# Head-by-head units, 128-token MLP chunks and two weights per unit in a clustered attention + MLP kernel

## The chip, the cores and the metric

The kernel runs on one core of a Trainium2 chip. That core has a matrix engine (PE, with its weight loads listed apart as PEld), a vector engine (DVE), a scalar engine (ACT), a general engine (POOL) and a queue engine (SP) that issues most transfers. The metric is the device time of one execution in microseconds. It is 1001.76 us before the change, the median of three runs.

## What is computed

```python
def _attn_ref(q, k, v, centroids):        # q, k, v: 4 x 8 x 768 x 64; centroids: 8 x 16 x 64
...
    q_assign = np.argmax(np.einsum('bhsd,hcd->bhsc', q_n, c_n), axis=-1)
    k_assign = np.argmax(np.einsum('bhsd,hcd->bhsc', k_n, c_n), axis=-1)
    mask = q_assign[:, :, :, None] == k_assign[:, :, None, :]
    scores = scale * np.matmul(q, k.transpose(0, 1, 3, 2))
    scores = np.where(mask, scores, -1000000000.0)
...
    return np.matmul(attn, v).astype(np.float32)      # attn: softmax of scores
def _moe_ref(x, w_in, w_out, s, b):       # x: 3072 x 512, w_in: 512 x 2048, w_out: 2048 x 512
    h = x @ w_in
    r = np.maximum(h, 0.0)
    g = s * (r * r) + b
    return (g @ w_out).astype(np.float32)
```

`q_n`, `k_n` and `c_n` are the rows divided by their norms. The attention output of the eight heads, put side by side, is `x`. The first function gives 24.6 thousand query rows against 768 keys each, the second is two large products.

## The kernel before

**Units.** A unit is 128 queries of one head against its 768 keys; there are 4 x 8 x 6 = 192. The list `units` runs over batch, chunk of 256 tokens (`c`), head pair (`hp`), 128-query tile in the chunk (`t`), head in the pair (`h`). So four units share a K pair before the next pair is touched, and one batch is 48 units in three chunks of 16. For each unit PE makes the scores (L462, two passes of two half rows: KA with QA, then KB with QB), DVE takes the row maximum (L471) and makes the bias of the exponential (L478), ACT takes the exponential (L481) and a 16-bit copy of it (L491), POOL subtracts that copy to get the low half (L504), a DMA transposes both halves, and five units later PE multiplies by V (L523 to L525; `px`). Numbers are kept as a high and a low fp16 half, and a product is three matmuls (high-high, high-low, low-high). The first 8 units use plain fp32, and so does the first MLP chunk.

**MLP.** A chunk of 256 tokens goes through 16 inner tiles of 128 columns (`ft`). Each unit has one step: `mlp_in` (L599, 12 matmuls of 256 columns), relu and two squares on ACT (L609, L615, L616), a subtraction on POOL (L628), and two units later `mlp_out` (L643, 6 matmuls of 512 columns into two accumulator banks). `LAG = 21` units lie between a unit and the MLP step of the same index, so a tail of MLP steps alone stands behind the last unit.

**Preparation.** K, Q and V are split into halves by generators that the loop steps once per unit. `prep_k` for batch b starts at unit 48b-20+4hp, `prep_v` at 48b-20, two `prep_q` per chunk 8 units apart. K: ACT writes the high half, DVE subtracts (L188) and copies the high half to `kb` (L332), a DMA transposes to KA; PE and DVE find the cluster of each row, written as a one-hot into `kb`, a second DMA transposes to KB. Q: the same with one scale per head pair, which takes a maximum over the partitions by way of PE (`allmax`, L98), two subtractions (L188) and a copy (L382) on DVE.

**Weights.** They come as 64-bit floats. `next(wgen)` at the end of a unit advances a four-step pipeline over 32 tiles (16 of w_in, 16 of w_out): load (`fetch`, SP), ACT rebases (L204, L206), DVE narrows (L210, L211), ACT or PE finds a bound (L217, L222) and POOL sets the sign (L224). `wsplit` then makes the fp16 halves, and the bound of all 16 tiles must be known for that.

**Order.** Python writes the program unit by unit; a list scheduler places the instructions on each engine's queue, and within a queue they run in order. In PSUM, scores have two pairs of banks, `acc` two banks, and the hidden bank `h` and the small bank `m` (`px`, `allmax`, `pk`, `pq`) one each. SBUF tiles of the tag `big` form one ring of 11.

Of the kernel before, what the change touches and what calls it, by code (L numbers as in the profile page):

```python
# [26 lines left out]
def tile_cluster_attention_mlp(ctx, tc, q, k, v, cent, w_in, w_out, s_in, b_in, out):  # L27
# [20 lines left out]
    URGENT = 20  # L48

# [5 lines left out]
    ps_m = ctx.enter_context(tc.tile_pool(name="ps_m", bufs=1, space=PSUM))  # L55
# [23 lines left out]
    last_exp = [None]  # L79

# [13 lines left out]
    def allmax(dst, src, name, bank="m"):  # L94
        n = src.shape[1]
        pm = (ps_m if bank == "m" else ps_h).tile([P, 512], F32, tag=bank, name=f"am_{name}")
        for j in range(n):
            nc.tensor.matmul(pm[:, j * P : (j + 1) * P], src[:, j : j + 1].broadcast_to([P, P]), identb, start=True, stop=True)  # L98
        V.tensor_reduce(dst, pm[:, : n * P].rearrange("p (n q) -> p n q", q=P), axis=AX.X, op=ALU.max)

# [78 lines left out]
    def split(hi, lo, src, f, early):  # L179
        if early:  # L180
            A.activation(src, src, AF.Copy, scale=f)
            last_split[1] = A.activation(hi, src, AF.Copy)
            yield
            G.tensor_tensor(lo, src, hi, op=ALU.subtract)
        else:
            last_split[1] = A.activation(hi, src, AF.Copy, scale=f)
            yield
            V.scalar_tensor_tensor(lo, src, f, hi, op0=ALU.mult, op1=ALU.subtract)  # L188
# [24 lines left out]

    def bound(d):
        w, p, ft = d["w"], d["p"], d["ft"]
        if p % 2:
            A.activation(w, w, AF.Abs, accum_out=l1[:, ft : ft + 1])  # L217
        else:
            wa = w.bitcast(BF16).rearrange("p a (f z) -> p a f z", z=2)[:, :, :, 1]
            pw = ps_h.tile([P, 512], F32, tag="h", name=f"pw_{ft}")  # L220
            for t in range(KT):
                nc.tensor.matmul(pw[:, :P], ones, wa[:, t, :], start=(t == 0), stop=(t == KT - 1))  # L222
# [40 lines left out]
    def wsplit(ft):  # L263
        while narrowed[0] < 2 * NF:
            next(wgen)
        made = []
        for w, f in ((wi[ft], glob[:, 2:3]), (wo[ft], glob[:, 5:6])):
            e = parts(weight_tile(f"w{'io'[len(made)]}s{ft}"))
            if made:
                A.activation(w, w, AF.Copy, scale=f)  # L270
                A.activation(e[:, 0], w, AF.Copy)
                G.tensor_tensor(e[:, 1], w, e[:, 0], op=ALU.subtract)
            else:
                A.activation(e[:, 0], w, AF.Copy, scale=f)
                yield
                V.scalar_tensor_tensor(e[:, 1], w, f, e[:, 0], op0=ALU.mult, op1=ALU.subtract)
            made.append(e)
        WSP[ft] = (made[0], made[1].rearrange("p e a f -> p e (a f)"))

    def column_sums():  # L280
# [5 lines left out]
        bias.append(weight_tile("bias").rearrange("p a f -> p (a f)"))  # L286
        V.tensor_scalar(bias[0], pb, glob[:, 7:8], None, op0=ALU.mult)
# [18 lines left out]
    kb_kept = const([P, 2, T, 2, D], F16, "kb")  # L306

    def prep_k(b, hp):
        kb = kb_kept
        if b == 0 and hp > 0:  # L310
            kb = sb.tile([P, 2 * T, P], F16, tag="big", name=f"kb_{hp}", bufs=BIGN).rearrange("p (h t) (e d) -> p h t e d", h=2, e=2)
        n = f"{b}_{hp}"
        kn = sb.tile([P, 2, T, D], F32, tag="kv", name=f"kn_{n}", bufs=5)
# [9 lines left out]
        allmax(sm[1], km, f"k{n}", "m" if b or not hp else "h")  # L323
# [8 lines left out]
        last_split[0] = V.tensor_copy(kb[:, :, :, 0, :], ka[:, :, :, 0, :])  # L332
# [6 lines left out]
        pa = (ps_m if b or not hp else ps_h).tile([P, 512], F32, tag="m" if b or not hp else "h", name=f"pk_{n}")  # L339
# [11 lines left out]
    def prep_q(b, c, hq):  # L351
        n = f"{b}_{c}_{hq}"
        nh = 4
        qn = sb.tile([P, 2 * T * P // 2], F32, tag="big", name=f"qn_{n}", bufs=BIGN)[:, : nh * CT * D].rearrange("p (h t d) -> p h t d", h=nh, t=CT)
        load(
            qn, q[b, nh * hq : nh * hq + nh].rearrange("h (p t) d -> p h t d", t=T)[:, :, c * CT : (c + 1) * CT, :]
# [3 lines left out]
        sm = sb.tile([P, 4, 2], F32, tag="qsm", name=f"qsm_{n}", bufs=3)  # L360
        qm = columns(2, f"q{n}")
        absmax(qm, qn.rearrange("p (j h) t d -> p j (h t d)", j=2))
        if b + c:
            yield
        allmax(sm[:, 1, :], qm, f"q{n}", "m" if b or c else "h")
# [7 lines left out]
        qb = sb.tile([P, 2 * T * P], F16, tag="big", name=f"qb_{n}", bufs=BIGN)[:, : nh * CT * 2 * D].rearrange("p (h t e d) -> p h t e d", h=nh, t=CT, e=2)
        both = []
        for j in range(2):
            hs = slice(2 * j, 2 * j + 2)
            both.append(split(qb[:, hs, :, 0, :], qa[:, hs, :, 0, :], qn[:, hs], sm[:, 2, j : j + 1], b + c == 0))
        for z in zip(*both):
            yield
        for z in both:  # L380
            next(z, None)
        V.tensor_copy(qa[:, :, :, 1, :], qb[:, :, :, 0, :])  # L382
        QA = sb.tile([P, nh * CT, P], F16, tag="QA", name=f"QA_{n}", bufs=2)
        QB = sb.tile([P, nh * CT, P], F16, tag="QB", name=f"QB_{n}", bufs=2)
# [422 lines left out]
```

## Time and profile before

| | us |
|---|---|
| runs | 997.03, 1001.76, 1005.69 |
| median | 1001.76 |
| profiled execution, its span | 998.5 |
| last exponential starts | 923.6 |

The profile is one execution: the busy time of each engine, a strip of 40 slices of the span, DMA queues, the chain of work that ended last, and the costliest groups of instructions. A group's row names line, engine, operation, what it writes and reads, its count, its busy time, the mean in ns of one, and the idle time before it with what ended that. A windows row gives start and end, length, then busy us and count of PE, PEld, DVE, ACT and POOL, the granted clock of PE as a share of full speed, the DMA share and GB/s. Rows for a source line alone have the busy time and count of that line instead of the engines. Busy PE is not PE at its peak: matmuls are pipelined, and a mean duration such as 276 ns for L599 is longer than the distance between two starts.

The DMA queues of the page show that small packets make up the traffic: 415760 of 448122 packets are under 512 B, and the queue took a 75.4% share of 16 engines' span.

### The profile page before, as it was taken

The page shows a single profiled execution, that of the slowest core. Times are in us where ns is not written, and L with a number is a line of the kernel's source. Part 1 is how long each engine was busy: PE and PEld are TensorE (multiplying, and loading weights), DVE is VectorE, ACT ScalarE, POOL GpSimd, SP SyncE. Part 2 cuts the span into 40 slices and gives each one's busy share as a digit, 9 for nine tenths or more (in the row PEclk, how much of TensorE's full clock was granted, in tenths as well). Part 3 has the DMA queues.
Part 4 walks back from the last instruction along what each step waited for, and adds up shares of the span by engine and source line. Part 5 has one row for each costly group of instructions (what it writes and reads, how often), then busy time and mean ns, then how long its engine had stood idle before and what let it go on. Part 6 is the DMA issues. An engine that isn't in the chain of part 4 may idle for free. (4 is left out here: it accounts for less than half of the span.)

```text
span 998.5 us, 22264 instructions
## 1 busy us (share of the span) xinstructions
PE 857.4 (86%) x8536; PEld 593.9 (59%) x8536; DVE 683.9 (68%) x1688; ACT 681.3 (68%) x1232; POOL 523.7 (52%) x498
## 2 busy tenths in 40 slices
PE   1487558978988999987899999987998998999997
PEld 0366345554655676654666666664666675767764
DVE  6887798887988567677878666588877577474100
ACT  3466678677777587765767777765877776777543
POOL 1115666534677366644456666553566565666321
PEclk9857579989999999998999999998999999999999
DMA  7855999966587787899697878898979868687300
GB/s 184 194 155 124 240 203 215 231 137 123 118 138 117 143 145 132 173 189 164 131 175 134 146 125 165 153 188 169 166 132 168 138 109 163 121 138 133 55 27 22
DMA packets 448122, 146.82 MB, mean 147 GB/s; under 512 B 415760, under 2 KB 444432, under 8 KB 448016
## 3 DMA queue, kind: packets, MB, share of 16 engines
q1 hardware_dynamic: 448016, 145.41, 75.4%
q8 instruction: 67, 1.10, 0.4%
q14 instruction: 39, 0.32, 0.1%
HBM read 35.69 MB, written 6.29 MB: 42 GB/s over the span
## 5 line engine op out<-in xcount | busy, mean ns | idle before, releaser
L504 POOL TENSOR_TENSOR ph<-p,ph 128x768 f16<-128x768 f32 x184 | 310.6, 1688 | 224.8 <-ACT ph L491 184.7
L599 PE MATMUL h<-x,wis 128*128 128x256 f16 x2112 | 268.3, 276 | 9.6 <-DMA x<-xn 5.9
L643 PE MATMUL acc<-wos,g 128*128 128x512 f16 x1056 | 272.8, 379 | 2.5 <-POOL g L628 2.2
L599 PEld LDWEIGHTS <-wis 128*128 128x128 f16 x2112 | 206.0, 99 | 62.1 <-issue 12.1
L481 ACT ACTIVATE p<-sc,ssm,qsm 128x768 f32<-128x768 f32 x192 | 188.6, 982 | 65.3 <-DVE ssm L478 35.2
L471 DVE TENSOR_REDUCE ssm<-sc 128x1 f32<-128x768 f32 x192 | 180.9, 949 | 27.1 <-PE sc L462 26.9
L628 POOL TENSOR_TENSOR g<-r,g 128x256 f16<-128x256 f32 x176 | 122.6, 697 | 108.5 <-ACT r L616 103.9
L609 ACT ACTIVATE r<-h,cf 128x256 f32<-128x256 f32 x176 | 82.5, 469 | 119.9 <-PE h L599 91.5
L491 ACT ACTIVATE ph<-p 128x768 f16<-128x768 f32 x184 | 153.1, 832 | 9.6 <-DMA PT<-ph 8.1
L523 PE MATMUL px<-vh,PT 128*128 128x65 f16 x1104 | 121.9, 198 | 25.4 <-DVE xs L537 8.6
L643 PEld LDWEIGHTS <-g 128*128 128x128 f16 x1056 | 94.8, 98 | 75.6 <-POOL g L628 5.4
L523 PEld LDWEIGHTS <-PT 128*128 128x128 f16 x1104 | 105.1, 99 | 30.1 <-issue 21.7
L524 PE MATMUL px<-vl,PT 128*128 128x64 f16 x1104 | 121.8, 195 | 0.0
L525 PE MATMUL px<-vh,PT 128*128 128x65 f16 x1104 | 121.5, 196 | 0.0
L462 PE MATMUL sc<-KA,QA 128*128 128x384 f16 x384 | 102.3, 345 | 21.4 <-ACT p L481 18.4
L524 PEld LDWEIGHTS <-PT 128*128 128x128 f16 x1104 | 104.8, 101 | 22.5 <-issue 14.4
L462 PE MATMUL sc<-KB,QB 128*128 128x384 f16 x384 | 101.4, 348 | 10.9 <-DMA QB<-qb 10.9
L525 PEld LDWEIGHTS <-PT 128*128 128x128 f16 x1104 | 104.9, 99 | 3.5 <-issue 0.9
L615 ACT ACTIVATE g<-r 128x256 f16<-128x256 f32 x176 | 72.8, 414 | 3.5
L616 ACT ACTIVATE r<-r 128x256 f32<-128x256 f32 x176 | 72.4, 412 | 3.3
L531 DVE TENSOR_SCALAR ssm<-px 128x2 f32<-128x2 f32 x92 | 14.1, 153 | 81.1 <-PE px L525 81.0
L462 PEld LDWEIGHTS <-QA 128*128 128x128 f16 x384 | 36.7, 103 | 48.4 <-issue 25.4
(163 smaller groups left out, 1189.8 us busy)
## 6 DMA issues: line engine op xcount, KB each, us to landing
wst<-in_moe_w_in_dram SPq DMA_DIRECT2D x16, 512.0 KB, 4.9
wst<-in_moe_w_out_dram SPq DMA_DIRECT2D x16, 512.0 KB, 4.4
kn<-in_k_dram SPq DMA_DIRECT2D x16, 384.0 KB, 3.9
qn<-in_q_dram SPq DMA_DIRECT2D x24, 256.0 KB, 3.8
vn<-in_v_dram SPq DMA_DIRECT2D x16, 384.0 KB, 4.2
out_dram<-o SPq DMA_DIRECT2D x12, 512.0 KB, 4.0
PT<-ph SPq DMA_TRANSPOSE x184, 4.0
x<-xn SPq DMA_TRANSPOSE x44, 2.8
```

The lines of the kernel that those rows point to most:

```text
L462: last_score[0] = nc.tensor.matmul(sc[:, e, :HALF], X[:, col, :], y[:, h * S + e * HALF : h * S + (e + 1) * HALF], start=st, stop=not st)
L471: last_max[0] = V.tensor_reduce(SM[i // 4][:, 0, j : j + 1], U[i]["sc"], axis=AX.XY, op=ALU.max, negate=True)
L481: last_exp[0] = A.activation(p.rearrange("p (a b) -> p a b", a=2), u["sc"], AF.Exp, bias=bi, scale=u["scale"], **total)
L491: A.activation(u["ph"][:, 0, :], u["p"], AF.Copy)
L504: G.tensor_tensor(u["ph"][:, 1, :], u["p"], u["ph"][:, 0, :], op=ALU.subtract)
L523: nc.tensor.matmul(o1, PT[:, kt, :], vh[:, h, kt, : D + 1], start=(kt == 0), stop=False)
L524: nc.tensor.matmul(o, PT[:, kt, :], vl[:, h, kt, :], start=False, stop=False)
L525: nc.tensor.matmul(o1, PT[:, T + kt, :], vh[:, h, kt, : D + 1], start=False, stop=(kt == T - 1))
L599: nc.tensor.matmul(ph[:, :CW], WSP[ft][0][:, wl, kt, :], XS[(b, c, kt)][:, :, xl, :], start=(i == 0), stop=(i == len(terms) - 1))
L609: A.activation(r, ph[:, :CW], AF.Relu, scale=MS[(b, c)][0])
L628: G.tensor_tensor(g[:, 1, :], r, g[:, 0, :], op=ALU.subtract)
L643: nc.tensor.matmul(acc[:, t, :], g[:, gl, rows], WSP[ft][1][:, wl, :], start=(ft == 0 and gl + wl == 0), stop=(ft == NF - 1 and gl == 1))
```

## The change

Units run in the order batch, 128-query tile, head pair, head: two units share a K pair, and all four pairs are wanted within 8 units. A batch has six tiles of 8 units; the two Q preparations for 256 tokens are started 4 units apart, every 16 units. An MLP chunk is one such tile of 128 tokens, so that a chunk's input is whole after 8 units. An MLP step (one per unit, eight per chunk) does two inner tiles: twice 12 matmuls of 128 columns, and 6 output matmuls of 512 columns as before. Four inner tiles share the bank `h`, and relu, squares and subtraction run once in two units over 512 columns. `LAG` is 14, the output stands 3 units behind (`BEHIND`), each chunk is written by itself (24 writes of 256 KB for 12 of 512 KB), and two chunks of 128 tokens are plain in place of one of 256.

```diff
-    LAG = 21
-    BIGN = 11
+    LAG = 14
+    BEHIND = 3
+    BIGN = 12
...
-    ps_m = ctx.enter_context(tc.tile_pool(name="ps_m", bufs=1, space=PSUM))
+    ps_m = ctx.enter_context(tc.tile_pool(name="ps_m", bufs=2, space=PSUM))
...
-    units = [(b, c, hp, t, h) for b in range(B) for c in range(NCH) for hp in range(NP) for t in range(CT) for h in range(2)]
+    units = [(b, t, hp, h) for b in range(B) for t in range(T) for hp in range(NP) for h in range(2)]
...
+        for j in range(2):
+            ft = 2 * m + j
+            o = ph[:, (2 * (m % 2) + j) * P :][:, :P]
...
+            for i, (kt, wl, xl) in enumerate(terms):
+                nc.tensor.matmul(o, WSP[ft][0][:, wl, kt, :], XS[(n, kt // 2)][:, kt % 2, xl, :],
+                                 start=(i == 0), stop=(i == len(terms) - 1))
...
+    def mlp_relu(n, m):
+        if m % 2 == 0:
             return
...
+        A.activation(r, ph, AF.Relu, scale=MS[n][0])
+        if not plain(n):
+            A.activation(g[:, 0, :], r, AF.Square)
+        A.activation(r, r, AF.Square)
```

The small bank `m` has two buffers, `acc` one, and the plain units' transposes go through `h` and `m`. In each unit two weight tiles are advanced, the second ahead of the low half of the exponential. A pair of weight tiles, a load's staging and the later batches' K rows are buffers of one ring (`slot`, 19 pairs). The bound of w_out is found by PE; `wsplit` makes w_out's halves on ACT and POOL for odd tiles, on DVE for even ones, and starts from unit 26 on, ten tiles in six units.

```diff
             mlp_in(*steps[m])
             mlp_relu(*steps[m])
+        next(wgen, None)
         if 0 <= i - 1 < NU:
             with first_of_all(i):
                 low(i - 1)
...
-        at(LAG + NF - 4 + ft, wsplit(ft))
+        at(LAG + 12 + (ft * 6) // 10, wsplit(ft))
```

The bias of the exponential moves from DVE to ACT. K's second copy of the high half moves to POOL. Q gets one scale per row (8 columns a preparation): no `allmax`, one multiplication on DVE, the copy and the subtraction on POOL. `until` holds a generator back to a unit.

```diff
-        V.tensor_scalar(bi, sm[:, 0, j : j + 1], u["scale"], LIFT, op0=ALU.mult, op1=ALU.add)
+        A.activation(bi, sm[:, 0, j : j + 1], AF.Identity, scale=u["scale"], bias=lift)
...
-        last_split[0] = V.tensor_copy(kb[:, :, :, 0, :], ka[:, :, :, 0, :])
+        last_split[0] = G.tensor_copy(kb[:, :, :, 0, :], ka[:, :, :, 0, :])
+        if b and hp:
+            yield from until(first - 8)
...
-        V.tensor_copy(qa[:, :, :, 1, :], qb[:, :, :, 0, :])
+        last_split[1] = A.activation(qb[:, :, 0, :], rows, AF.Copy)
+        yield
+        G.tensor_copy(qa[:, :, 1, :], qb[:, :, 0, :])
+        last_split[0] = G.tensor_tensor(qa[:, :, 0, :], rows, qb[:, :, 0, :], op=ALU.subtract)
...
-                at(48 * b - 20 + 4 * hp, prep_k(b, hp))
-            at(48 * b - 20, prep_v(b))
+                at(PERB * b - 15 + 2 * hp, prep_k(b, hp))
+            at(PERB * b - 24, prep_v(b))
```

SP's queue during the first units, before. `wst` are loads of weights, `qn` of Q; KB_2 and KB_3 are the second K transposes of head pairs 2 and 3 of batch 0, QB_0_1 the second Q transpose that these pairs need:

```order
L86 DMA wst_633<-in_moe_w_out_dram 128x1024
L349 DMA_TRANSPOSE KB_2_371<-kb_140 128x12x128
L86 DMA wst_684<-in_moe_w_in_dram 128x4x256
L349 DMA_TRANSPOSE KB_3_376<-kb_143 128x12x128
L86 DMA wst_728<-in_moe_w_out_dram 128x1024
L86 DMA qn_1_0_716<-in_q_dram 128x4x128
L86 DMA wst_781<-in_moe_w_in_dram 128x4x256
L399 DMA_TRANSPOSE QB_0_1_382<-qb_0_1_242 128x8x128
```

The same place now:

```order
L90 DMA wst_531<-in_moe_w_out_dram 128x1024
L90 DMA wst_552<-in_moe_w_in_dram 128x4x256
L90 DMA wst_613<-in_moe_w_out_dram 128x1024
L90 DMA wst_634<-in_moe_w_in_dram 128x4x256
L90 DMA wst_659<-in_moe_w_out_dram 128x1024
L363 DMA_TRANSPOSE KB_2_356<-kb_2_214 128x12x128
L409 DMA_TRANSPOSE QB_0_1_366<-qb_0_1_231 128x8x128
```

Head pair 2 is reached at unit 4 instead of 8; its two transposes stand behind a run of weight loads instead of between them.

VectorE in a Q preparation in the middle of the program, before. `qsm` are its scales, `qn` the rows of Q, `qa` and `qb` the 16-bit halves:

```order
L369 TENSOR_TENSOR qsm_1_0_7724<-qsm_1_0_7724,ksm_0_5696 128x2
L370 TENSOR_TENSOR qsm_1_0_7724<-qsm_1_0_7724,ksm_0_5696 128x2
L65 TENSOR_SCALAR qsm_1_0_7724<-qsm_1_0_7724 128x2
L188 SCALAR_TENSOR_TENSOR qa_1_0_7864<-qn_1_0_7642,qsm_1_0_7724,qb_1_0_7865 128x4x64 x2
L382 COPY qa_1_0_7864<-qb_1_0_7865 128x8x64
```

And now (the last row already belongs to a unit's attention result, `px`):

```order
L383 TENSOR_TENSOR qsm_1_0_8527<-qsm_1_0_8527,ksm_0_6670 128x8
L384 TENSOR_TENSOR qsm_1_0_8527<-qsm_1_0_8527,ksm_0_6670 128x8
L386 TENSOR_TENSOR qn_1_0_8436<-qn_1_0_8436,qsm_1_0_8527 128x512
L68 TENSOR_SCALAR qsm_1_0_8527<-qsm_1_0_8527 128x8
L539 TENSOR_SCALAR ssm_7922<-px_8487 128x2
```

The subtractions and the copy have left VectorE's queue, and one multiplication of all 512 elements has come in.

More of the change, by code (lines that the diff above doesn't have):

```diff
@@ L322, in prep_k @@
             yield
-        allmax(sm[1], km, f"k{n}", "m" if b or not hp else "h")
+        allmax(sm[1], km, f"k{n}")
         yield
@@ L359, in prep_q @@
         prs = slice(2 * hq, 2 * hq + 2)
[L360 to L365, printed above, removed]
+        sm = sb.tile([P, 4, m], F32, tag="qsm", name=f"qsm_{n}", bufs=4)
+        rows = qn.rearrange("p h t d -> p (h t) d")
+        absmax(sm[:, 1, :], rows)
         yield
@@ L373, in prep_q @@
[L373 to L382, printed above, removed]
@@ new lines, in mlp_g, with mlp_out @@
+    def mlp_g(n, m):
+        if m % 2 == 0:
+            return
+        s = m // 2
+        r, g = GS[(n, s)]
+        if plain(n):
+            V.tensor_scalar(r, r, sv, bv, op0=ALU.mult, op1=ALU.add)
+            GS[(n, s)] = r
+        else:
+            G.tensor_tensor(g[:, 1, :], r, g[:, 0, :], op=ALU.subtract)
+            GS[(n, s)] = g
+    def mlp_out(n, m):
+        if m == 0:
+            MS[n][2] = ps_a.tile([P, DM], F32, tag="acc", name=f"acc_{n}")
+        _, scale, acc = MS[n]
+        g = GS[(n, m // 2)]
+        for j in range(2):
+            ft = 2 * m + j
+            rows = slice((2 * (m % 2) + j) * P, (2 * (m % 2) + j + 1) * P)
+            if plain(n):
+                nc.tensor.matmul(acc, g[:, rows], wo[ft].rearrange("p a f -> p (a f)"), start=(ft == 0), stop=(ft == NF - 1))
@@ L641, in mlp_out @@
                 continue
             for gl, wl in ((0, 0), (0, 1), (1, 0)):
[L643 removed]
+                nc.tensor.matmul(acc, g[:, gl, rows], WSP[ft][1][:, wl, :],
                                  start=(ft == 0 and gl + wl == 0), stop=(ft == NF - 1 and gl == 1))
[L645 to L655 removed]
@@ L658, in tile_cluster_attention_mlp @@
-    steps = [(b, c, ft) for b in range(B) for c in range(NCH) for ft in range(NF)]
+        if m % 2:
+            del GS[(n, m // 2)]
+        if m == STEPS - 1:
+            del MS[n]
+            o = sb.tile([P, DM], F32, tag="o", name=f"o_{n}", bufs=1)
+            if plain(n):
+                V.tensor_copy(o, acc)
+            else:
+                if plain(n - 1):
+                    column_sums()
+                V.scalar_tensor_tensor(o, acc, scale, biased, op0=ALU.mult, op1=ALU.add)
+            b, t = n // T, n % T
+            nc.sync.dma_start(out[b * S : (b + 1) * S].rearrange("(p t) e -> p t e", t=T)[:, t, :], o)
@@ L659, in tile_cluster_attention_mlp @@
+    steps = [(n, m) for n in range(B * T) for m in range(STEPS)]
     NS = len(steps)
@@ L743, in tile_cluster_attention_mlp @@
     i = 0
-    while i < NU + 8 or i - LAG < NS + 4:
+    while i < NU + 8 or i - LAG < NS + BEHIND + 2:
         m = i - LAG
+        unit[0] = i
         prepare(i)
```

339 lines of the change are left out of this document (155 added, 184 removed).

## Prediction

> **What bounds the kernel now.** First the page: busy shares say which engines can matter at all.
>
> ```profile
> PE 857.4 (86%) x8536; PEld 593.9 (59%) x8536; DVE 683.9 (68%) x1688; ACT 681.3 (68%) x1232; POOL 523.7 (52%) x498
> ```
>
> PE leads, but 86% is a mean over stages, so next the start of the units in the group of exponentials (one per unit, 192) and the busy times by stage.
>
> ```profile
> L481 ACT ACTIVATE p<-sc,ssm,qsm x192: 968/982/997, 36.6 to 923.6; 128x768 f32<-128x768 f32 x192
> ```
>
> ```profile
> 119.00:303.90 184.90, 31.35 (x32) 0.92 0.80 167
> 303.90:923.60 619.70, 140.50 (x144) 0.98 0.83 149
> ```
>
> These two rows count the exponentials of a stretch: 32 and 144. So units 0 to 15 end at 119 us, units 16 to 47 (the rest of batch 0) at 303.9, units 48 to 191 at 923.6, and behind them stands an MLP tail. The busy table over the same stretches (columns: length; PE, PEld, DVE, ACT, POOL busy; granted clock; DMA share, GB/s):
>
> ```profile
> 0.00:119.00 119.00, 66.65 (x483) 49.61 (x484) 90.01 (x243) 65.68 (x115) 37.12 (x58) 0.74 0.73 177
> 100.00:150.00 50.00, 28.90 (x318) 20.30 (x315) 43.16 (x92) 34.83 (x60) 30.67 (x21) 0.67 1.02 221
> 119.00:303.90 184.90, 151.16 (x1333) 101.34 (x1332) 155.93 (x358) 140.00 (x250) 105.73 (x85) 0.92 0.80 167
> 303.90:923.60 619.70, 570.95 (x6156) 396.23 (x6154) 430.12 (x1064) 441.37 (x792) 359.59 (x328) 0.98 0.83 149
> 923.60:998.50 74.90, 68.61 (x570) 46.69 (x568) 7.83 (x27) 34.29 (x79) 21.24 (x29) 0.99 0.15 35
> 437.00:520.00 83.00, 71.13 (x783) 49.29 (x781) 66.36 (x164) 57.08 (x99) 42.83 (x39) 0.94 0.85 156
> 587.00:653.00 66.00, 63.58 (x676) 44.70 (x675) 41.32 (x107) 48.22 (x89) 37.88 (x35) 1.00 0.78 151
> 653.00:737.00 84.00, 73.82 (x824) 50.52 (x821) 69.03 (x173) 56.04 (x98) 44.12 (x41) 0.96 0.90 166
> ```
>
> Three regimes. Up to 304 us VectorE is the fullest engine (90.0 of 119, 155.9 of 184.9 = 84%). In the middle, blocks of 16 units last 66 us with PE full (63.6), except the two blocks before a new batch (437 to 520, 653 to 737), which last 83 and 84: there VectorE rises to 66 and 69 us for the K, V and Q preparation, and PE falls to a clock of 0.94 and 0.96. The tail is matmul after matmul, as the chain of work that ended last shows:
>
> ```profile
> 984.43 1.29 PE acc L643 x6
> 985.73 1.31 PE h L599 x12
> 987.04 1.29 PE acc L643 x6
> ```
>
> From it come prices: 12 hidden-layer matmuls of 256 columns take 1.31 us (109 ns each), 6 output matmuls of 512 columns 1.29.
>
> **Part 1, twice as many matmuls in mlp_in.** Chunks of 128 tokens make of 2112 matmuls of 256 columns 4224 of 128, each with its own weight load. The columns are the same; the question is whether a load hides behind 128 columns.
>
> ```profile
> 603.25 0.19 PE L525 MATMUL px<-vh,PT 128*128 128x65 f16 x1
> 603.28 0.19 PE L523 MATMUL px<-vh,PT 128*128 128x65 f16 x1
> 835.47 0.28 PE L98 MATMUL am_q<-identb,amb_q 128*128 128x128 bf16 x2 [1.98 <-DVE amb_q L102]
> 611.31 0.22 PE L98 MATMUL am_x<-identb,amb_x 128*128 128x128 bf16 x1
> ```
>
> The px matmuls, 65 columns, each with a load of its own, start 30 ns apart, so a load adds at most that. Two L98 matmuls of 128 columns with their loads take 0.28 us where one takes 0.22: 60 ns apart. Against half of 109 that is up to 5 ns more for each; the half itself (54.5) is the floor. I take 56, nearer to the floor, since 30 ns of load fits twice behind it: 4224 x 1.5 = **+6 us** (ends 0 and +23). This counts in full, PE being the bound where most of them run.
>
> The Trainium skill, "TensorE: Matmul & The Clock Gate", section "Back-to-back issue gap", speaks against the change: a stream of load-and-multiply pairs sustains about 81 ns per matmul at 128 columns and 131 at 512. By it mlp_in would cost 4224 x 25 = 106 us more than by my price. Here the trace disagrees at both ends, with 30 ns for px and 1.29/6 = 215 ns for 512 columns.
>
> **Part 2, a shorter lag.** Before, the MLP step is 21 units behind and its output 2 more; now 14 and 3. Behind the last unit stand 7 fewer hidden steps (1.31) and 6 fewer output steps (1.29): 9.2 + 7.7 = **-17 us** of tail. The work does not vanish: it moves to units 14 to 20, where PE was idle (66.7 busy of 119, at a clock of 0.74). If that cover were gone it would be paid there, so the ends are -17 and 0. I take -17.
>
> **Part 3, two weights per unit.** All 32 weight tiles are to be narrowed before the second half of batch 0. What comes first is seen on SP's queue, the only one that loads; its order in the section on the change ends with QB_0_1, which the third head pair needs: at unit 8 before, at unit 4 now.
>
> More loads of weights stand ahead of a transpose that is wanted earlier. By unit 16 the order has 30 weights narrowed where it had 16. The prices:
>
> ```profile
> L210 DVE TENSOR_SCALAR wi<-wi 128x512 int32<-128x512 int32 x16 | 7.6, 476 | 4.1 <-ACT wi L204 4.1
> L211 DVE SCALAR_TENSOR_TENSOR wi<-wst,wi 128x512 uint32<-128x512 uint32 x16 | 17.3, 1084 | 0.1
> L211 DVE SCALAR_TENSOR_TENSOR wo<-wst,wo 128x512 uint32<-128x512 uint32 x16 | 10.9, 682 | 0.1
> L224 POOL TENSOR_TENSOR wi<-wi,wsg 128x512 f32<-128x512 f32 x16 | 20.0, 1251 | 35.1 <-PE pw L222 15.1 <-DVE oe_q L298 10.4 <-PE am_k L98 4.4
> L206 ACT ACTIVATE wsg<-wst 128x512 bf16<-128x512 f32 x32 | 21.1, 661 | 5.0 <-POOL wi L224 3.6 <-POOL wo L224 1.4
> ```
>
> For 14 weights: VectorE 14 x (0.48 + 0.88) = 19 us, ScalarE 14 x 2 x 0.66 = 19, POOL 14 x 1.25 = 18, and the queue 14 x 524 KB at the 221 GB/s of the fullest row = 33 us. VectorE stood idle 29 of 119 us and the queue 32, so the lower end is 0; a queue already at 0.73 x 119 = 87 us plus 33, if it again idles as much as before, gives +33. The queue is the tighter of the two and in between I take **+18 us** for units 0 to 15.
>
> Units 16 to 47 then have less for VectorE: 19 us of narrowing gone, and of part 4 the bias (32 x 0.21 = 7); new there are 16 operations that split w_out (8 scalings, 8 subtractions, 12 us), against 8 fewer g operations. A count of all its rows gives 23 us less. At the same 84% that is about -27 us; PE, with 147 us of column time there by the order, would at 92% allow -25. I take **-25** (ends 0, if something else paces it, and -30).
>
> **Part 4, lighter VectorE in the blocks before a batch, two small banks.** What goes and what it cost:
>
> ```profile
> L478 DVE TENSOR_SCALAR ssm<-ssm,qsm 128x1 f32<-128x1 f32 x192 | 38.2, 206 | 1.4
> L188 DVE SCALAR_TENSOR_TENSOR qa<-qn,qsm,qb 128x256 f16<-128x256 f32 x44 | 34.3, 816 | 5.5 <-ACT r L609 3.1 <-DMA PT<-ph 2.4
> L382 DVE COPY qa<-qb 128x512 f16<-128x512 f16 x24 | 20.7, 862 | 0.0
> L332 DVE COPY kb<-ka 128x768 f16<-128x768 f16 x16 | 15.5, 975 | 5.0 <-DMA KB<-kb 5.0
> L523 PE MATMUL px<-vh,PT 128*128 128x65 f16 x1104 | 121.9, 198 | 25.4 <-DVE xs L537 8.6 <-DVE xm L99 5.0 <-DVE qsm L99 4.9
> ```
>
> In a Q preparation (VectorE's order in the section on the change) two subtractions and a copy became one multiplication of 128x512. Per block before a batch VectorE loses 16 x 0.21 for the bias, 2 x (2 x 0.82 + 0.86) for Q and 4 x 0.98 for K, 12.2 us; it gains 2 x about 0.9 (an estimate from L211's two rows, the same 512 elements) and one more chunk's small chain, about 1.5: 9 us less of 66 to 69. At the 80% that it is busy there this is 11 us per block, and PE's need (66) stops it at 17. I take -10 each, **-20 us** (ends 0 and -34).
>
> The waits of L523 on DVE reductions (xm, qsm) are waits for the one small bank that px, am, pk and pq shared. With two, I book **-4 us** for the blocks without preparation (ends 0 and -10).
>
> POOL takes over 40 copies and 24 subtractions, 1 to 1.3 us each by L224's row: some 60 us on 524, to 59%, hidden while units take 4 us and it has one 1.69 us subtraction in each. ScalarE pays 192 bias operations (0.2) and loses more by wide MLP activations: 128x256 cost 469, 414 and 412 ns, 128x512 661 by L206, so three per two units cost 2.0 for 2.6 us. Off the path.
>
> ```profile
> L609 ACT ACTIVATE r<-h,cf 128x256 f32<-128x256 f32 x176 | 82.5, 469 | 119.9 <-PE h L599 91.5 <-DVE xm L583 9.3 <-DVE cf L582 8.3
> L615 ACT ACTIVATE g<-r 128x256 f16<-128x256 f32 x176 | 72.8, 414 | 3.5
> L616 ACT ACTIVATE r<-r 128x256 f32<-128x256 f32 x176 | 72.4, 412 | 3.3
> L504 POOL TENSOR_TENSOR ph<-p,ph 128x768 f16<-128x768 f32 x184 | 310.6, 1688 | 224.8 <-ACT ph L491 184.7 <-issue 22.4 <-PE px L525 5.6
> ```
>
> **The sum.** 998.5 + 6 - 17 + 18 - 25 - 20 - 4 = 956.5 us for the profiled execution. The median of the runs before lies 3.3 above its span (1001.76), so 960.
>
> **Rivals.** (a) The blocks before a batch fall to PE's 66 us: 14 more, 946, or 940 with the other terms at their good ends; for it speaks PE's 63.6 of 66 elsewhere. (b) They stay at 83, since four K pairs are now wanted within 8 units and not 16: 980. (c) The early weights are not repaid: +18 stays and -25 goes, 985; with (b), 1005, no change. For it: SP's order. Against: VectorE's 84% in that stretch. (d) Slower, by the K preparation: a block now loses 18 us to it; squeezed into half the units it loses twice that, three times 18 more than in (b), 980 + 54 = 1034. It decides from some 7 us per transition beyond (b). VectorE's lighter load speaks against it. (e) Slower, by weight loads not hidden: at the 99 ns that L599's loads are shown to take, 4224 x 43 = 182 more, 1142; it turns the result from 66 ns per matmul on. The px spacing speaks against it.
>
> ```profile
> L599 PEld LDWEIGHTS <-wis 128*128 128x128 f16 x2112 | 206.0, 99 | 62.1 <-issue 12.1 <-DVE wis L276 0.3
> ```
>
> By the skill's 81 ns, (e) would end at 1066.
>
> **How the numbers follow.** Forecast 0.46, (a) 0.12, (b) 0.15, (c) 0.06 as faster and 0.07 with (b) as no change, (d) 0.06, (e) 0.04; 0.04 unexplained, half of it faster, one quarter each the others. About 1% (10 us) is what a measurement of this kernel can tell from no change. Faster: 0.46 + 0.12 + 0.15 + 0.06 + 0.02 = 0.81; same 0.08; slower 0.11. The range 932 to 990 holds the forecast, (a), (b) and (c) alone.
>
> **What would show it.** The 128-column matmuls of mlp_in start 56 ns apart, not 66. Unit 16 starts near 137 us and unit 48 near 297. The blocks before batches 2 and 3 last some 73 us. The tail behind the last exponential is 57 us. A unit 48 behind 320, or blocks over 90, would make the forecast wrong.

## The result and the profile after

The changed kernel takes 1013.49 us (median of six runs, 1007.26 to 1016.4) against 1002.49 us before: a ratio of 1.010, 95% interval 1.0063 to 1.0136. It is slower by one per cent, where 960 had been forecast. The profiled execution spans 1012.9 us, 14.4 more than before. Stage times below come from one profiled execution each; that of e3 was a slow one (1010.4 us at a median of 1006.5), so its stages are if anything too long.

The page after, the group of exponentials, and the group of output matmuls (L657; its idle time and what ended it stand last):

```profile
PE 861.0 (85%) x10753; PEld 636.0 (63%) x10754; DVE 625.7 (62%) x1520; ACT 670.9 (66%) x1060; POOL 566.7 (56%) x471
```

```profile
L490 ACT ACTIVATE p<-sc,ssm,qsm x192: 970/990/995, 41.0 to 962.1; 128x768 f32<-128x768 f32 x192
```

```profile
L657 PE MATMUL acc<-ws,g 128*128 128x512 f16 x1056 | 272.6, 383 | 30.2 <-DVE o L669 21.3 <-POOL g L642 8.6 <-ACT g L629 0.2
```

VectorE is lighter by 58 us, as intended, and PE's busy time is the same within 4 us. New is the last row: PE stands 30.2 us ahead of output matmuls, 21.3 of it until L669 has run. L669 is the eviction: VectorE reads the accumulator, and only then can the next chunk write that bank. Before, with two banks, the row of the output matmuls had 2.5 us:

```profile
L643 PE MATMUL acc<-wos,g 128*128 128x512 f16 x1056 | 272.8, 379 | 2.5 <-POOL g L628 2.2
```

By stages (units 0 to 15, 16 to 47, the two blocks before batches 2 and 3, the tail):

```profile
0.00:144.70 144.70, 75.55 (x527) 55.87 (x529) 117.83 (x254) 79.90 (x137) 64.78 (x80) 0.79 0.75 198
144.70:327.70 183.00, 160.18 (x1766) 115.44 (x1765) 136.15 (x308) 115.73 (x187) 111.01 (x81) 0.93 0.70 130
464.80:547.10 82.30, 72.09 (x995) 54.23 (x993) 55.80 (x143) 55.26 (x88) 47.51 (x39) 0.94 0.87 162
685.10:769.90 84.80, 71.74 (x994) 54.28 (x993) 55.94 (x144) 55.40 (x88) 46.59 (x38) 0.94 0.91 162
962.10:1012.90 50.80, 45.62 (x565) 32.71 (x563) 6.61 (x23) 17.67 (x28) 12.53 (x12) 1.00 0.18 38
```

Put beside the stages before, with unit 80 at 440.1 and 464.8, unit 128 at 657.7 and 685.1:

| stage | before | after | difference | forecast |
|---|---|---|---|---|
| to unit 16 | 119.1 | 144.7 | +25.6 | +18 |
| units 16 to 47 | 184.9 | 183.0 | -1.9 | -25 |
| blocks 80 to 95 and 128 to 143 | 163.9 | 167.1 | +3.2 | -20 |
| the other units from 48 on | 455.7 | 467.3 | +11.6 | +2 (128 columns +6, bank -4) |
| behind the last exponential | 74.9 | 50.8 | -24.1 | -17 |
| span | 998.5 | 1012.9 | +14.4 | -42 |

### The profile page after: what moved, and what is told of

It is laid out like the page before. It is cut to its first block, busy times and chain, and to the rows that moved or that the text cites. A ratio compares the mean times of both kernels' runs of the same rounds, so it can differ in the third digit from the quotient of the medians.

```text
span 1012.9 us, 26350 instructions
## 1 busy us (share of the span) xinstructions
PE 861.0 (85%) x10753; PEld 636.0 (63%) x10754; DVE 625.7 (62%) x1520; ACT 670.9 (66%) x1060; POOL 566.7 (56%) x471
## 4 chain that ended last, share of the span: by engine, by line
PE 36%; DVE 13%; DMA 10%; issue 9%; POOL 8%; ACT 3%; SPq 1%; POOLq 0%; ACTq 0%; DVEq 0%
PE h L614 13%; PE acc L657 12%; PE sc L471 4%; POOL ph L512 3%; DMA qn<-in_q_dram 3%; DVE ssm L480 3%; POOL g L642 2%; PE px L531 2%; DMA PT<-ph 2%; PE px L533 2%; PE px L532 2%; DMA kn<-in_k_dram 1%; DVE ws L279 1%; ACT ph L498 1%; SPq L514 1%
## 5 line engine op out<-in xcount | busy, mean ns | idle before, releaser
L614 PEld LDWEIGHTS <-ws 128*128 128x128 f16 x4224 | 263.4, 100 | 57.4 <-issue 13.8
L657 PE MATMUL acc<-ws,g 128*128 128x512 f16 x1056 | 272.6, 383 | 30.2 <-DVE o L669 21.3
L614 PE MATMUL h<-x,ws 128*128 128x128 f16 x4224 | 284.5, 223 | 9.4 <-ACT r L627 6.3
L487 ACT ACTIVATE ssm<-ssm,lift,qsm 128x1 f32<-128x1 f32 x192 | 73.6, 383 | 159.8 <-DVE ssm L480 157.8
L657 PEld LDWEIGHTS <-g 128*128 128x128 f16 x1056 | 97.8, 98 | 113.6 <-issue 23.8
L642 POOL TENSOR_TENSOR g<-r,g 128x512 f16<-128x512 f32 x88 | 105.8, 1202 | 36.7 <-ACT r L630 22.4
L531 PE MATMUL px<-vh,PT 128*128 128x65 f16 x1104 | 118.0, 197 | 8.2 <-DMA PT<-ph 2.4
L532 PE MATMUL px<-vl,PT 128*128 128x64 f16 x1104 | 117.4, 194 | 0.0
L533 PE MATMUL px<-vh,PT 128*128 128x65 f16 x1104 | 117.1, 195 | 0.0
L627 ACT ACTIVATE r<-h,cf 128x512 f32<-128x512 f32 x88 | 59.9, 681 | 38.3 <-PE h L614 36.3
L231 POOL TENSOR_TENSOR w<-w,wsg 128x512 f32<-128x512 f32 x32 | 41.0, 1292 | 58.8 <-PE pw L229 28.0
L471 PEld LDWEIGHTS <-QB 128*128 128x128 f16 x384 | 38.6, 102 | 37.0 <-DMA QB<-qb 13.0
```

The source lines that it names most:

```text
L471: last_score[0] = nc.tensor.matmul(sc[:, e, :HALF], X[:, col, :], y[:, h * S + e * HALF : h * S + (e + 1) * HALF], start=st, stop=not st)
L487: A.activation(bi, sm[:, 0, j : j + 1], AF.Identity, scale=u["scale"], bias=lift)
L531: nc.tensor.matmul(o1, PT[:, kt, :], vh[:, h, kt, : D + 1], start=(kt == 0), stop=False)
L532: nc.tensor.matmul(o, PT[:, kt, :], vl[:, h, kt, :], start=False, stop=False)
L533: nc.tensor.matmul(o1, PT[:, T + kt, :], vh[:, h, kt, : D + 1], start=False, stop=(kt == T - 1))
L614: nc.tensor.matmul(o, WSP[ft][0][:, wl, kt, :], XS[(n, kt // 2)][:, kt % 2, xl, :], start=(i == 0), stop=(i == len(terms) - 1))
```

## The experiments

All start from the changed kernel unless the text says otherwise. The table gives the median, the 95% interval of the ratio to the kernel before (measured again beside each group of runs), and from each profiled execution the start of units 16 and 48, the time from there to the last exponential (batches 1 to 3) and the tail.

| run | us | ratio to before | unit 16 | unit 48 | batches 1-3 | tail |
|---|---|---|---|---|---|---|
| before | 1002.5 | | 119 | 304 | 620 | 75 |
| changed | 1013.5 | 1.006-1.014 | 145 | 328 | 634 | 51 |
| e1 two accumulator banks | 1026.8 | 1.020-1.026 | 148 | 332 | 642 | 51 |
| e2 late first output | 1006.4 | 1.000-1.004 | 145 | 316 | 638 | 50 |
| e3 copies back on VectorE | 1006.5 | 0.997-1.006 | 153 | 325 | 632 | 51 |
| e4 three weights in two units | 1001.5 | 0.997-1.002 | 131 | 319 | 633 | 51 |
| e5 lag 16 | 1017.4 | 1.011-1.021 | 145 | 320 | 639 | 55 |
| e6 lag 16, later am_x | 1007.5 | 1.002-1.006 | 145 | 321 | 632 | 55 |
| e7 ring of 11 | 1013.1 | 1.007-1.013 | 145 | 326 | 636 | 52 |
| e8 e2 and e4 | 1012.4 | 1.006-1.016 | 128 | 325 | 635 | 50 |
| e9 lag 21 | 1001.5 | 0.995-1.000 | 146 | 321 | 607 | 69 |
| e10 before, two weights | 1009.8 | 1.004-1.008 | 132 | 307 | 621 | 76 |
| e11 no K preparation | 965.4 | 0.959-0.965 | 145 | 320 | 594 | 51 |
| e12 slack, lag 16 | 986.8 | 0.981-0.987 | 135 | 307 | 625 | 55 |
| e13 eight buffers of x | 1011.6 | 1.004-1.010 | 146 | 332 | 632 | 51 |
| e14 lag 22 | 1026.5 | 1.018-1.027 | 145 | 314 | 643 | 72 |
| e15 slack, lag 21 | 1004.4 | 0.997-1.003 | 134 | 309 | 621 | 69 |
| e16 slack, lag 18 | 1017.7 | 1.007-1.016 | 136 | 318 | 636 | 61 |
| e17 lag 15 | 976.7 | 0.971-0.977 | 145 | 323 | 605 | 52 |
| e18 lag 15 and e4 | 974.0 | 0.970-0.975 | 131 | 317 | 601 | 52 |

**The accumulator's eviction (e1, e2).** First, two accumulator banks for one, paid for with the second small bank (the bound of w_out is then summed in an accumulator bank throughout):

```diff
-    ps_a = ctx.enter_context(tc.tile_pool(name="ps_a", bufs=1, space=PSUM))
+    ps_a = ctx.enter_context(tc.tile_pool(name="ps_a", bufs=2, space=PSUM))
-    ps_m = ctx.enter_context(tc.tile_pool(name="ps_m", bufs=2, space=PSUM))
+    ps_m = ctx.enter_context(tc.tile_pool(name="ps_m", bufs=1, space=PSUM))
```

> The changed kernel with two accumulator banks and one small bank again; nothing else. Theory A: the single accumulator bank makes the first output matmul of a chunk wait for the eviction of the chunk before (in the changed kernel nine such waits, 21.3 us of PE, ended by L669); with two banks they go, and the time falls by 14 to 21 us to 992 to 999. The second small bank, which I had booked at -4, would give back at most 4 of it. Rival B: PE would have waited there for something else (scores, px), then the waits appear under other names and the time stays within 5 us of 1013; or the second small bank is worth more than the waits, and it is slower.

Its rows of the output matmuls and of two users of the small bank:

```profile
L657 PE MATMUL acc<-ws,g 128*128 128x512 f16 x1056 | 270.4, 382 | 13.3 <-POOL g L642 11.5 <-POOL vh L447 1.3 <-ACT g L629 0.2
L531 PE MATMUL px<-vh,PT 128*128 128x65 f16 x1104 | 112.0, 195 | 23.2 <-DVE xs L545 10.0 <-DVE ksm L103 6.6 <-DVE xm L103 5.2
L405 PE MATMUL pq<-cT,QA 128*128 128x16 f16 x192 | 12.9, 171 | 26.0 <-DVE xs L545 14.1 <-DMA QA<-qa 11.3 <-ACT PT L124 0.6
```

The waits on L669 are gone, and 13 us are lost all the same: px and pq now wait on VectorE (xs, ksm, xm) until the one small bank is read out. The second small bank is worth more here than what the second accumulator bank gives; my -4 for it was far too small.

The second edit left the banks alone:

```diff
+        late = 0 <= m - BEHIND < NS and steps[m - BEHIND][1] == 0
-        if 0 <= m - BEHIND < NS:
+        if 0 <= m - BEHIND < NS and not late:
             mlp_out(*steps[m - BEHIND])
...
+        if late:
+            mlp_out(*steps[m - BEHIND])
         background()
```

> The changed kernel with the first output step of each chunk written at the end of its unit instead of near its start; banks as in the changed kernel. Theory A: the eviction then has half a unit (about 2 us) more, the L669 waits of 2.4 us shrink below 1 us, and the time falls by 8 to 18 us to 995 to 1005. Rival B: the order on PE is not what makes it wait, the time stays within 5 us of 1013.

The output row's L669 wait fell from 21.3 to 1.5 us, and am_x, PE's part of the maximum over x, took its place (its wait on L573 was 3.0 us in the changed kernel):

```profile
L657 PE MATMUL acc<-ws,g 128*128 128x512 f16 x1056 | 270.0, 385 | 12.6 <-POOL g L642 11.1 <-DVE o L669 1.5
L102 PE MATMUL am_x<-identb,amb_x 128*128 128x128 bf16 x22 | 5.0, 229 | 17.0 <-DVE amb_x L573 14.6 <-DVE oe_q L303 2.4
```

Batches 1 to 3 took as long as before the edit (638 for 634). The 7 us came in batch 0. So moving one wait out of PE's way did not free PE: the next wait at a chunk's end took its place, and all of PE's pauses over 30 ns in batches 1 to 3 add up to 53 us instead of 55.

**VectorE in the blocks (e3, e11).**

```diff
-        last_split[0] = G.tensor_copy(kb[:, :, :, 0, :], ka[:, :, :, 0, :])
+        last_split[0] = V.tensor_copy(kb[:, :, :, 0, :], ka[:, :, :, 0, :])
...
-        G.tensor_copy(qa[:, :, 1, :], qb[:, :, 0, :])
-        last_split[0] = G.tensor_tensor(qa[:, :, 0, :], rows, qb[:, :, 0, :], op=ALU.subtract)
+        V.tensor_copy(qa[:, :, 1, :], qb[:, :, 0, :])
+        last_split[0] = V.tensor_tensor(qa[:, :, 0, :], rows, qb[:, :, 0, :], op=ALU.subtract)
```

> The changed kernel with K's copy and Q's copy and subtraction back on VectorE: some 7 us more VectorE work in each 16-unit block before a batch. Theory A (blocks are paced by PE's own extra work, its stalls and its clock, not by VectorE): blocks from unit 80 to 96 and 128 to 144 stay at 82 to 85 us, within 3, and the total within 5 us of 1013. Rival B (my prediction's reading: VectorE at 80% sets their length): each gets 9 us longer, three of them 27 us, 1040.

The two blocks of e3, and then those of e11, in which batches 1 to 3 use batch 0's K and its scales:

```profile
466.10:544.30 78.20, 69.20 (x967) 50.47 (x965) 60.54 (x155) 54.81 (x86) 38.92 (x31) 0.96 0.96 164
682.70:762.90 80.20, 69.62 (x957) 50.92 (x955) 63.40 (x155) 54.95 (x85) 38.68 (x31) 0.94 0.93 161
```

```diff
-        ks = [KSM[b][:, e, prs].unsqueeze(2).broadcast_to([P, 2, m // 2]) for e in range(4)]
+        ks = [KSM[0][:, e, prs].unsqueeze(2).broadcast_to([P, 2, m // 2]) for e in range(4)]
...
-        KA, KB = KS[(b, hp)]
+        KA, KB = KS[(0, hp)]
...
-            for hp in range(NP):
-                at(PERB * b - 15 + 2 * hp, prep_k(b, hp))
```

> The changed kernel without the K preparation of batches 1 to 3, which use the K of batch 0 (so the output of those batches is another one): price of that preparation. A block before a batch lasts 82 to 85 us, a pair of blocks without it 137, 68.6 each. Theory A (PE's own extra work and its in-order waits make the difference): the blocks from 80 to 96 and 128 to 144 fall by 6 to 12 us, the time by 20 to 40 to 973 to 993, with V and Q preparation left. Rival B (VectorE sets them, 4 x 2.5 us of K work in each at 80%): 13 us each or more, to below 72.

```profile
454.70:522.60 67.90, 64.77 (x900) 48.57 (x897) 40.77 (x97) 52.36 (x83) 43.55 (x35) 1.00 0.76 137
655.60:725.90 70.30, 65.72 (x899) 48.81 (x898) 39.98 (x101) 52.47 (x83) 43.36 (x35) 1.00 0.75 133
```

With 5 to 7 us more on VectorE the blocks of e3 are 4 us shorter, not 9 longer, and its median is 7 us below the changed kernel, not 27 above: VectorE's load does not set them. Without the K preparation they fall by 14 us, to 68 and 70, while PE's busy time falls by 6 to 7 and the granted clock rises from 0.94 to 1.00. By its size alone e11 meets the rival's number (below 72), and its 965.4 us lie outside theory A. With e3 against that rival, PE's own work, its waits and its clock are what is left; this is by exclusion, since no run takes one of them away alone.

**Weights (e4, e8, e10).** The second advance only in odd units; the same together with e2; and the kernel before with the second advance alone:

```diff
-        next(wgen, None)
+        if i % 2:
+            next(wgen, None)
```

> The changed kernel with three weights in two units instead of four; all are narrowed by unit 21 instead of 16. Theory A (batch 0 lasts as long as all its work takes together, wherever it lies): unit 16 starts some 8 us earlier than 145, unit 48 within 5 us of 328, the time within 5 us of 1013. Rival B (the burst of weights itself stalls PE and VectorE, and what it costs is not paid back): unit 48 starts 8 to 15 us earlier and the time falls by as much.

> Three weights in two units and the late first output step together. If both act on batch 0 by their own: 1013 - 12 - 7 = 994, unit 48 near 310. If both take away the same waits in batch 0: 1000, unit 48 near 317.

> The kernel before with two weights per unit and nothing else of the change. Theory A (the burst costs units 0 to 15 some 20 us and is not paid back, because what holds units 16 to 47 is not VectorE's narrowing): unit 16 at 130 to 140 instead of 119, unit 48 at 314 to 324 instead of 304, the time 1012 to 1022. Rival B (my prediction's: paid back by unit 48): unit 48 at 297 to 305, the time 995 to 1003.

In e4, which drops half of the second advances, unit 16 starts 14 us earlier and unit 48 still 9: about a third of what they cost is paid back in the changed kernel. In the kernel before, 13 us by unit 16 become 3.5 by unit 48, between the two theories, and its time is 0.6% longer. With e2 the gain of e4 does not add up at all: unit 48 is back at 325, later than with either edit alone and outside both expectations.

**The large ring and the buffers of x (e7, e13).** `BIGN` 11 for 12, and that with 8 buffers of x for 5:

```diff
-    BIGN = 12
+    BIGN = 11
...
-        x = sb.tile([P, 2, 2, P], F16, tag="x", name=f"x_{g}", bufs=5)
+        x = sb.tile([P, 2, 2, P], F16, tag="x", name=f"x_{g}", bufs=8)
```

> The changed kernel with 11 buffers of the large ring instead of 12. Theory A (that ring, which now also holds kb of every head pair and r, is short and sets the pace in the blocks before a batch): those blocks grow by 5 us or more from 82 to 85, the time by 15 or more to 1028. Rival B (the ring is not short): within 5 us of 1013.

> The changed kernel, lag 14, with 8 buffers of x for 5 and 11 of the large ring. Theory A (lag 21 gained by its lag): within 5 us of 1013, batches 1 to 3 at 630 to 640 us. Rival B (the buffers of x were short): 985 to 1000, batches 1 to 3 near 607.

Both are within 2 us of the changed kernel: neither is short.

**The lag (e5, e6, e9, e12, e14 to e18).** First two units more, then also a `yield` between the reduction of x's maximum (L573) and its am_x matmul:

```diff
-    LAG = 14
+    LAG = 16
...
             V.tensor_reduce(xc, xm[:, 0:2], axis=AX.X, op=ALU.max)
+            yield
             allmax(xm[:, 5:6], xc, f"x{g}")
```

> The changed kernel with the MLP 16 units behind instead of 14. Theory A (a shorter lag only moves MLP steps from the tail into batch 0, where they are paid for): two steps of 2.6 us go back, the tail behind the last exponential gets 5 us longer than its 51, unit 48 starts 4 to 8 us earlier than 328, and the time stays within 4 us of 1013. Rival B (my prediction's: the steps are free in batch 0): 5 us slower, 1018, unit 48 unmoved.

> As the run with 16 units of lag, and the maximum over the partitions of a chunk's x (am_x on PE) is written one unit after the VectorE reduction that it waits for. Theory A (each chunk's end makes PE wait in order, and twice as many chunks mean twice as many such waits): am_x waits vanish, 3 to 10 us less than the run with the lag alone. Rival B (PE's waits are replaced by others of the same size, since another ring sets the pace): within 3 us of it, with some 50 us of waits on PE between unit 48 and the last exponential as in every run so far.

Lag 16 starts unit 48 8 us earlier, as theory A had it, but batches 1 to 3 got 5 us longer. The `yield` took 10 us off the time, although PE's waits for a free scores bank rose from 4 to 16 us. Then the lag of the kernel before (`LAG` 21, with the buffers of e13):

> The changed kernel with the MLP 21 units behind, as before the change; three more buffers of x, and 11 of the large ring to make room (a run with 11 alone took 1013.1). Theory A (the moved steps are paid in batch 0): unit 48 starts 15 to 24 us earlier than 328, at 304 to 313, the tail is 7 x 2.6 = 18 us longer than 48, and the time stays within 6 us of 1013. Rival B (my prediction: PE was idle there, the steps were free): unit 48 at 325 to 330, the tail 18 us longer, 1031.

Neither theory had this: unit 48 only 6 us earlier than in the changed kernel (10 than in e13, which has the same buffers), the tail 18 longer, and batches 1 to 3 shorter by 28 us (25 against e13). Slack for several waits at once, at lag 16 (with the weights of e4, the `yield` of e6, and one more at two places of `prep_k` and one of `prep_q`):

```diff
         if b:
             yield
+            yield
         allmax(sm[1], km, f"k{n}")
...
         last_turn[0] = nc.sync.dma_start_transpose(KA, ka.rearrange("p h t e d -> p (h t e d)"))
+        if b:
+            yield
...
         nc.sync.dma_start_transpose(QA, qa.rearrange("p n e d -> p (n e d)"))
+        if b + c:
+            yield
```

> The changed kernel with three weights in two units, the MLP 16 units behind, the maximum of x one unit after its reduction, and one unit more between the transposes of Q and K and the matmuls that read them. If PE's in-order waits on late inputs cost what they show, most of 49 us between unit 48 and the last exponential goes and the weights give 10 back: 985 to 995, faster than both kernels. If other waits take their place: 997 to 1005.

It beat both kernels, though PE's pauses in batches 1 to 3 hardly fell, from 55 to 47 us, under other names; lag 21 had 32. Most of its gain lies in batch 0: unit 48 starts 21 us earlier, batches 1 to 3 are 10 us shorter. To find what lag 21 had done, one more unit, and two lags with the slack of e12 (all three with the buffers of e13):

> As the run with lag 21, one unit more, so that a chunk's end falls at the same place in the 8 units of a tile as with 14. Theory A (room between x and its step decides): batches 1 to 3 at 600 to 612 us, few waits on the eviction, 1001 to 1007 with 2.6 us more tail. Rival B (the place in the tile decides): waits on the eviction as with 14, batches 1 to 3 at 628 to 640, 1020 to 1035.

> Lag 21 with three weights in two units and the slack of the twelfth run. If lag and slack act on different waits: unit 48 near 307 as in that run, batches 1 to 3 near 605, tail 66: 975 to 985, faster than both kernels. If on the same waits: 995 to 1002.

> The same with lag 18: three steps of 2.6 us less in the tail, 58. If room decides, and 18 is room enough: batches 1 to 3 near 607, 975 to 985. If the place in the tile decides, between 985 (batches 1 to 3 at 625, as with lag 16 and slack) and 1000.

Slack and lag 21 did not add: e15 came out near its second theory, with 621 us in batches 1 to 3 where lag 21 alone has 607, and e16 (1017.7) above both of its own. Lag 22 is no faster in batches 1 to 3 than 14 (643 for 634), and its output row reads alike, while that of lag 21 is nearly empty. Here are lag 22, lag 21 and lag 15:

```profile
L657 PE MATMUL acc<-ws,g 128*128 128x512 f16 x1056 | 273.0, 384 | 32.1 <-DVE o L669 20.4 <-POOL g L642 11.4 <-ACT g L629 0.2
```

```profile
L657 PE MATMUL acc<-ws,g 128*128 128x512 f16 x1056 | 268.0, 382 | 3.1 <-POOL g L642 1.3 <-DVE o L669 1.1 <-ACT g L629 0.7
```

```profile
L657 PE MATMUL acc<-ws,g 128*128 128x512 f16 x1056 | 267.4, 382 | 3.8 <-POOL g L642 3.7
```

Lag 22 leaves more room than 21, so room is not it. The last two runs asked for odd against even:

```diff
-    LAG = 14
+    LAG = 15
```

> The changed kernel with a lag of 15 for 14 and nothing else. Theory A (with an odd lag a chunk's last output step falls in a unit in which VectorE has no attention result of a pair to scale): the eviction follows the last accumulation by less than 0.5 us in the mean, batches 1 to 3 at 605 to 615, tail 2.6 us longer, 985 to 995. Rival B (only the place that 21 has, or its room, helps): batches 1 to 3 at 630 to 640, 1010 to 1018.

> Lag 15 and three weights in two units. If both gains hold, unit 48 is some 9 us earlier than with lag 15 alone: 975 to 986, faster than both kernels. If they do not add, as with the late first output step: 990 to 1000.

One unit of lag takes 37 us: lag 15 runs in 976.7 us, 2.6% faster than the kernel before (interval 0.971 to 0.977), and with the slower weights in 974.0. The timeline shows what this unit moves. First lag 14, around the end of a chunk (start, length, engine, line):

```profile
577.70 1.64 POOL L512 TENSOR_TENSOR ph<-p,ph 128x768 f16<-128x768 f32 x1 [2.41 <-ACT ph L498]
577.83 1.54 DVE L72 TENSOR_SCALAR qsm<-qsm 128x8 int32<-128x8 int32 x1
...
578.12 1.03 PE L657 MATMUL acc<-ws,g 128*128 128x512 f16 x4
...
579.30 1.15 POOL L642 TENSOR_TENSOR g<-r,g 128x512 f16<-128x512 f32 x1
...
579.40 1.08 DVE L73 TENSOR_SCALAR qsm<-qsm 128x8 int32<-128x8 int32 x1
579.47 1.50 PE L614 MATMUL h<-x,ws 128*128 128x128 f16 x24
...
581.01 0.69 DVE L386 TENSOR_TENSOR qn<-qn,qsm 128x512 f32<-128x512 f32 x1
...
581.76 0.95 DVE L480 TENSOR_REDUCE ssm<-sc 128x1 f32<-128x768 f32 x1
...
583.02 0.74 DVE L669 SCALAR_TENSOR_TENSOR o<-acc,xm,biased 128x512 f32<-128x512 f32 x1
583.67 0.41 DVE L106 TENSOR_REDUCE xm<-xs 128x1 f32<-128x256 f32 x1
583.81 0.59 PE L657 MATMUL acc<-ws,g 128*128 128x512 f16 x2 [2.50 <-DVE o L669]
```

Then lag 15:

```profile
597.20 1.24 PE L657 MATMUL acc<-ws,g 128*128 128x512 f16 x5
...
598.28 0.19 PE L531 MATMUL px<-vh,PT 128*128 128x65 f16 x1
...
598.48 0.75 DVE L669 SCALAR_TENSOR_TENSOR o<-acc,xm,biased 128x512 f32<-128x512 f32 x1 [0.20 <-PE acc L657]
...
598.70 1.50 PE L614 MATMUL h<-x,ws 128*128 128x128 f16 x24
...
601.36 0.59 PE L657 MATMUL acc<-ws,g 128*128 128x512 f16 x2
```

With lag 14 PE has the scores and one hidden step (1.50 us) between the last output matmul of a chunk and the first of the next; VectorE still has a Q preparation, a maximum and an attention result ahead of the eviction, and PE stands for 2.50 us with everything behind it. With lag 15 the px matmuls of a pair (from 598.28 on) also lie between, and the eviction runs at once. Attention results come in odd units only, so an odd lag puts a chunk's last output into a unit with px behind it. (The expectation of e17 put it the other way round, as a unit without an attention result.)

The traces of lags 14 and 22 show that px alone is not the reason. At lag 14, 17 chunks end in batches 1 to 3, each in an even unit and with no px before the next output, yet only nine make PE wait for the eviction. Eight of these waits, 2.1 to 2.9 us each, stand at every second chunk end, from unit 56 to unit 168 in steps of 16, where the first of two Q preparations makes its scales. Lag 22 has its eight waits, 2.0 to 3.1 us, at the same eight units. At unit 184 no Q preparation is left, and neither lag has a wait there. Of the other chunk ends one waits, for 0.96 us at lag 14. Here is one that does not, with the same lag and no px:

```profile
614.49 1.46 PE L657 MATMUL acc<-ws,g 128*128 128x512 f16 x6
615.78 1.50 PE L614 MATMUL h<-x,ws 128*128 128x128 f16 x24
615.82 0.88 DVE L305 TENSOR_TENSOR oe_q<-oe_q,rev 128x128 f32<-128x128 f32 x1
...
616.62 0.74 DVE L669 SCALAR_TENSOR_TENSOR o<-acc,xm,biased 128x512 f32<-128x512 f32 x1
...
618.28 1.46 PE L657 MATMUL acc<-ws,g 128*128 128x512 f16 x6
```

So lag 14 lets a chunk's end meet a Q preparation on VectorE, and lag 15 moves it one unit behind those scales and puts px in between, both at once. No run moves the Q preparation alone. In the chunk shown first, L72 and L73 take 1.54 and 1.08 us under POOL's subtractions, ending 0.03 us behind them, instead of 0.15 each (last section). That is 2.3 us more, nearly PE's 2.50; that the wait would go without it is an estimate from these rows, which no run tests.

## Why the prediction was wrong, point by point

Of the 56 us between the forecast span (956.5) and the measured one (1012.9), the early weights' repayment and the lighter blocks make 23 each, the other units 10 and the first 16 units 8; the tail came out 7 better. The mechanism that both large terms rest on, VectorE as the engine that sets a stage, failed. That is the case of rivals (b) and (c) together, 1005 at a chance of 0.07, with some 8 us more. The largest price found by a run, that of the lag's place among the units, stood in no term.

**128-column matmuls, +6: right in its price.** Stretches such as this one from the chain of waits give 1.34/24 = 56 ns:

```profile
904.92 1.34 PE h L614 x24
```

The Trainium skill ("TensorE: Matmul & The Clock Gate", "Back-to-back issue gap") gives 81 ns for such a stream; the trace disagrees with its 56, and rival (e) is out.

**The lag, -17 with its cover: the tail right, the rest failed.** The tail did get shorter, by 24 us, 7 more than booked. But I took the lag as a shift of work and nothing else. It also sets where a chunk's end falls among the units. An accumulator of one bank instead of two makes PE wait at that place, 24 chunks have twice as many of them, and that bank was not in my sum at all. Lag 15 for 14 takes 29 us out of batches 1 to 3 (634 to 605), and PE's waits there fall from 55 to 30. That the wait on the eviction alone is worth those 29 us is not shown: e2 took 20 us of it away and gained nothing in these batches. Batch 0 hid little of the moved steps: against e13, with the same buffers, lag 21 starts unit 48 10 us earlier and lag 22 17, of 18 and 21 us moved (2.6 us a step). These starts are uncertain by some us: the changed kernel, e7 and e13 have 328, 326 and 332. That 976.7 lies in the forecast range is luck, since the terms of the sum did not come out so.

**Early weights, +18 and -25.** The first was near (+25.6, of which 4.4 us stand ahead of the first unit); of the second nothing came. Three weights in two units show that half of the second advances costs 14 us by unit 16 and 9 by unit 48. I had let VectorE set units 16 to 47 at 84%. Its work there did fall, from 156 to 136 us, but the stage kept its length and VectorE's idle time grew from 29 to 47 us, more than half of it ended by PE's px and scores (us, times, longest, from 144.7 to 327.7):

```profile
DVE ssm L539 <- PE px L533: 12.9, 6, 4.2
DVE ssm L480 <- PE sc L471: 12.4, 6, 3.5
```

PE itself was busy for 160 of these 183 us, before for 151 of 185.

**Blocks before a batch, -20: wrong in its mechanism.** Cut at the units' own starts, the two blocks before lasted 84.1 and 79.8 us; the second window of the prediction, 84 us, was 4 us too long for 16 units.

```profile
440.10:524.20 84.10, 70.78 (x784) 49.19 (x783) 66.07 (x162) 55.97 (x99) 44.14 (x40) 0.94 0.87 159
657.70:737.50 79.80, 69.62 (x775) 47.48 (x773) 65.33 (x164) 53.66 (x96) 43.45 (x40) 0.96 0.90 163
```

VectorE fell from 66 and 65 us to 56 and the blocks took 82 and 85, near rival (b), 83; e3 shows that VectorE's load does not pace them. A full engine in a stage was taken for its limit, without a wait that ends on it.

**Second small bank, -4: mis-sized.** Trading it for a second accumulator bank makes the kernel 13 us slower, even though this takes away the eviction's 21 us of waits.

Still open is what makes batch 0 longer by 24 us as a sum: half of the burst (9), the moved steps (10 and 17, when 7 or 8 are put back) and the late start (4) were each seen, but e8 shows that such gains do not add. Odd lags are only two, 15 and 21, and with the slack lag 21 loses most of its gain; what takes it away is not found. Of the even lags 14 and 22 have the eviction's waits; at 16 most of the time goes to other waits on PE (pq and am_x, 15 us each). The -29 us are shown for the one unit of lag; how they divide between the Q preparation, px and what follows from both is argued from the timelines.

## What to carry to other kernels

A lag between two pipelines is a phase as well as a distance: where a stage's single buffer turns over, look at what the producer has to do between its last write and its next, and try the neighbouring values before anything else. When PSUM banks are traded, price the bank that is given up by what turns over in it, not only the one that is won. Before a busy engine is taken for what sets a stage, look for waits that end on it: here 10 us less of VectorE work in a block gained nothing.

## What the runs showed of the hardware

Small VectorE operations were stretched by a running POOL operation. L73, on 128x8, takes 0.154 us at the least, but here 1.60 us, and it ends 25 ns behind the POOL subtraction that had begun before it:

```profile
499.09 1.64 POOL L512 TENSOR_TENSOR ph<-p,ph 128x768 f16<-128x768 f32 x1 [0.44 <-ACT ph L498]
499.15 1.60 DVE L73 TENSOR_SCALAR qsm<-qsm 128x8 int32<-128x8 int32 x1
```

Of its 24 instances the 11 that began under a POOL operation took 0.92 to 1.61 us and ended 25 to 31 ns behind it, and the other 13 took 0.15 to 0.17. The Trainium skill ("SBUF — State Buffer", "Who interferes with whom") has the two engines share a pair of ports; in VectorE's two-port modes, which `tensor_scalar` can enter, the one that issues first holds it for a whole instruction and the other is blocked. The trace agrees in these 11 instances; it does not show which mode L73 ran in. So work moved from VectorE to POOL can be paid for in part on VectorE. That is one reason why e3, with those copies back, could be faster; no run separates it from the others.
